# A Nyström attention and MLP kernel: its prologue re-ordered on all engines, W1 split over two engines, each output store cut into two of 64 rows

## The chip, the cores and the metric

The kernel runs on one NeuronCore of a Trainium2 chip. The metric is the device time of one execution in microseconds (us), as the median of several runs. The profile is of one further execution; times inside it count from the start of its span.

## The reference, cut to what matters

q, k and v are [8 batches, 8 heads, 576 rows, 64]. Each head uses 32 landmark rows (means over 18 rows) and a six-step iteration for an inverse; the eight heads' results are joined to x of [8, 576, 512], on which a layer norm and an MLP work.

```python
A, Bm, C = sm(q, k_lm), sm(q_lm, k_lm), sm(q_lm, k)
for _ in range(6):
    Z = 2 * Z - Z @ Bm @ Z
attn = A @ Z @ C @ v
...
xn = (x - mu) / np.sqrt(var + 1e-06) * g_ln
ch = np.maximum(xn @ w_ch1, 0.0) @ w_ch2
return x + ch
```

w_ch1 (W1) is [512, 2048] and w_ch2 (W2) is [2048, 512].

## The kernel before, in words

**Attention.** `attention(b)` is a generator: it emits one batch's attention in pieces and yields between them. Its inputs come by six loads of 576 KB each on SP's queue (`load`: q and k for two sets of four heads, then v), are cast to fp16 (`nat`, `natv`; by DVE, ACT and POOL for batch 0, by POOL for the rest), transposed on PE into `pst` and copied out as `xT`; `pss` holds the landmark sums (nine matmuls against the 0/1 matrix `pm16`). From `pss` DVE makes `klm` and `qbd`. Then come `psb` (landmark scores), its exponential `ebm`, the normalised `bm16`, its transpose `bmT`, then `psc`/`ect`, `psse`/`cmx`, `pscv`, six iterations of `psn` on PE and `st` on DVE (two `psa`/`ea` beside them), `pszc`, the two `zcbd`, and last five blocks of rows: `psy` on PE, `rcpd` and `xblk` on DVE. `block_done` takes the statistics of each finished block of 128 rows (`st6`, `mvg`) and, when four are there (a group), the layer norm: `lnv` and `rstd` on ACT, then four `xn`.

**MLP.** `mlp()` is a second generator, one step for each matmul. For each of nine groups it transposes `xn` (`psxt`, copied out by DVE as `xnT`), does 64 matmuls `psh` (16 column tiles of W1, `hT` is their ReLU, by ACT) and 64 matmuls `pso`; DVE adds x (`ot`), and `store` sends 256 KB to DRAM by one DMA, or two of 64 rows where a batch boundary falls into the block.

**Order.** PE runs in exactly the order written: the main loop takes one piece of attention, then `fill` takes some MLP matmuls. Batch 1's attention (`a1`) begins inside that of batch 0 (`a0`). The other engines' order comes from the scheduler, except DMA issues, which are pinned by `keep_in_program_order`. ACT, DVE, POOL and SP each run their list in order, so what waits holds what is behind it. W1 arrives in eight column blocks of 512 KB through `w1stg` (two buffers) on SP's queue, and ACT multiplies each by g in four operations (line 172); W2 arrives by four DMAs on POOL's queue that cast on the way (line 176). `psM` is a pool of three PSUM banks for `psh`, `pso`, `psxt` and, for one batch, the small attention tiles.

Of the kernel before, what the change touches and what calls it, by code (L numbers as in the profile page):

```python
# [15 lines left out]
P = 128  # L16
# [3 lines left out]
def kernel(  # L20
# [37 lines left out]

    def MM(o, l, r, rb=0, cb=0, start=True, stop=True, skip=False):
# [16 lines left out]
    def cast(eng, out_, in_):  # L76
        if eng == "act":
            nc.scalar.activation(out_, in_, AF.Copy)
        elif eng == "dve":
            nc.vector.tensor_copy(out=out_, in_=in_)  # L80
        else:
            nc.gpsimd.tensor_copy(out=out_, in_=in_)  # L82


    def load_qk(b, engines):
        tiles = {}
        for u in range(U):
            for (nm, src) in (("q", q), ("k", k)):
                tiles[nm, u] = load(src, b, u)
        out_ = {}  # L90
        for key, eng in zip(tiles, engines):
            t = nat.tile([P, NJ, 2, D], FP16, name="nat", tag="nat")
            cast(eng, t[:].rearrange("p j r d -> p r j d"), tiles[key][:])
            out_[key] = t
        return out_

    def load_v(b, engines):
        natv = natv_buf[b % NV]
# [66 lines left out]
    w1_stg = []  # L165

    def load_w1(i):
        stg = wstage.tile([P, KCH, W1N], FP32, name="w1stg", tag="w1stg")
        tc.keep_in_program_order(
            nc.sync.dma_start(out=stg[:], in_=w1_src[:, :, ts(i, W1N)]))  # L170
        for c in range(KCH):
            nc.scalar.activation(w1_16[:, c, ts(i, W1N)], stg[:, c, :], AF.Copy,  # L172
                                 scale=g_sb[:, c:c + 1])
# [30 lines left out]
    def attention(b):  # L204
        nt = nat_tiles.pop(b)
        natv = v_tiles.pop(b)
        zcbd = zcbd_buf[b % NV]
        pool1, tag1 = (psM, "pm") if b == 1 else (ps1, "p1")
# [44 lines left out]
        ebm = asm.tile([P, U, LM], FP32, name="ebm", tag="ebm")  # L253
        nc.scalar.activation(ebm[:], psb[:], AF.Exp, scale=sc_B)
# [13 lines left out]
        for u in range(U):  # L268
# [6 lines left out]
            nc.scalar.activation(t[:], psc[:], AF.Exp, scale=sc_C)  # L275
# [3 lines left out]
        psse = p1([P, 2, U, LM], "psse")  # L279
# [242 lines left out]
```

## Time and profile before

| | us |
|---|---|
| median of 3 runs (lowest, highest) | 393.53 (393.42, 395.13) |
| the profiled execution's own time | 391.23 |
| its span | 389.5 |
| PE busy in the span | 344.7 (89%) |
| DVE, ACT, POOL busy | 170.0, 129.7, 82.1 |

The span is what the trace covers; 1.73 us of the execution lie around it. PE is the busy engine, but a share over the whole span hides three stretches: a prologue in which PE mostly waits, a long stretch in which it hardly does, and an end without PE.

### The profile page before, as it was taken

What the parts mean: (1) busy time and instruction counts of PE and PEld (TensorE: products, weight loads), DVE (VectorE), ACT (ScalarE), POOL (GpSimd) and SP (SyncE); (2) the same over time, 40 slices, a digit from 0 to 9 for tenths busy, and PEclk for the clock granted to TensorE, in tenths of its full rate; (3) what the DMA queues carried; (4) which work ended last, traced back from release to release, by engine and by line L of the source; (5) the groups of instructions that cost most, each with busy time, mean ns of one, the idle gap of its engine ahead of it and who ended that gap; (6) DMA issues with size and microseconds to landing.
All of it is one profiled execution on the core that took longest, in us unless ns stands there. A gap on an engine that the chain in (4) does not pass through costs nothing.

```text
span 389.5 us, 8220 instructions
## 1 busy us (share of the span) xinstructions
PE 344.7 (89%) x3528; PEld 175.7 (45%) x3528; DVE 170.0 (44%) x431; ACT 129.7 (33%) x240; POOL 82.1 (21%) x100
## 2 busy tenths in 40 slices
PE   1796299799999999999999999999999999999940
PEld 1663045344554464446444644464444444444410
DVE  0548368635734574466347634852491210210110
ACT  2325854410551046014601450255027016016000
POOL 2750048500090009003600350300030210000000
PEclk9998679999999999999999999999999999999985
DMA  7999499201821191019111900100020011020011
GB/s 294 395 216 245 161 334 393 74 15 53 316 95 29 45 339 65 21 51 354 52 46 33 364 34 26 51 34 3 29 60 22 14 51 44 14 72 23 14 51 42
DMA packets 24755, 44.55 MB, mean 114 GB/s; under 512 B 1680, under 2 KB 7824, under 8 KB 24720
## 3 DMA queue, kind: packets, MB, share of 16 engines
q1 hardware_dynamic: 22608, 41.95, 30.5%
q0 software_dynamic: 2112, 2.10, 3.4%
q8 instruction: 27, 0.44, 0.5%
q14 instruction: 8, 0.07, 0.0%
HBM read 36.70 MB, written 9.44 MB: 118 GB/s over the span
## 4 chain that ended last, share of the span: by engine, by line
PE 82%; DVE 6%; DMA 4%; ACT 2%; issue 1%; POOL 1%; SPq 0%
PE pso L61 33%; PE psh L61 31%; PE pst L66 5%; DMA w1stg<-in_moe_w_ch_dram 2%; PE pss L61 2%; PE psn L61 2%; PE psy L61 2%; PE psxt L66 2%; ACT w L172 2%; DMA stg<-in_q_dram 2%; PE psa L61 2%; DVE ot L459 1%; DVE bm L260 1%; PE pscv L61 1%; PE psc L61 1%
## 5 line engine op out<-in xcount | busy, mean ns | idle before, releaser
L448 ACT ACTIVATE hT<-psh 128x512 f16<-128x512 f32 x144 | 85.7, 597 | 159.8 <-PE psh L61 159.8
L61 PE MATMUL psh<-xnT,w 128*128 128x512 f16 x576 | 137.5, 380 | 0.2 <-DVE xnT L427 0.2
L61 PE MATMUL pso<-w,hT 128*128 128x512 f16 x576 | 135.8, 380 | 0.2 <-DVE xnT L427 0.2
L61 PEld LDWEIGHTS <-hT 128*128 128x128 f16 x576 | 53.1, 98 | 60.2 <-issue 3.3
L61 PEld LDWEIGHTS <-w 128*128 128x128 f16 x576 | 52.9, 98 | 54.8 <-issue 2.1
L459 DVE TENSOR_TENSOR ot<-pso,xblk 128x512 f32<-128x512 f32 x36 | 24.8, 689 | 80.5 <-PE pso L61 80.5
L402 POOL TENSOR_SCALAR xn<-xblk,rstd,negmr 128x512 f16<-128x512 f32 x34 | 26.2, 785 | 138.2 <-DVE negmr L397 62.9
L82 POOL CAST nat<-stg 128x1152 f16<-128x1152 f32 x29 | 32.9, 1148 | 88.1 <-DMA stg<-in_q_dram 49.8
L324 DVE SCALAR_TENSOR_TENSOR st<-st,psn 128x192 f16<-128x192 f16 (+1 forms) x48 | 16.4, 342 | 48.6 <-PE psn L61 48.6
L66 PE MATMUL pst<-ident,nat 128*128 128x128 f16 x288 | 24.6, 239 | 6.7 <-DVE nat L80 5.4
L231 DVE COPY xT<-pst 128x1152 f16<-128x1152 f16 x28 | 21.1, 755 | 19.2 <-PE pst L66 19.2
L367 DVE TENSOR_TENSOR xblk<-psy,rcpd 128x512 f32<-128x512 f32 (+1 forms) x40 | 27.3, 684 | 0.7
L66 PEld LDWEIGHTS <-nat 128*128 128x128 f16 x288 | 20.9, 107 | 13.5 <-DVE nat L80 5.4
L388 DVE BATCH_NORM_STATS2 st<-xblk 128x6 f32<-128x512 f32 x36 | 24.5, 681 | 0.4
L82 POOL CAST natv<-stg 128x1152 f16<-128x1152 f32 x16 | 18.3, 1153 | 3.7 <-DMA stg<-in_v_dram 3.7
L66 PE MATMUL psxt<-ident,xn 128*128 128x128 f16 x144 | 12.9, 228 | 6.5 <-DVE xn L402 4.1
L61 PE MATMUL pss<-pm,nat 128*128 128x64 f16 x288 | 15.4, 204 | 3.5 <-POOL pm L114 3.5
L61 PE MATMUL psy<-zcbd,ea 128*128 128x260 f16 (+1 forms) x80 | 16.3, 287 | 1.8 <-DVE xblk L367 1.2
L338 ACT ACTIVATE ea<-psa 128x576 f16<-128x576 f32 x16 | 10.4, 650 | 18.3 <-PE psa L61 18.3
L172 ACT ACTIVATE w<-w1stg,g_sb 128x256 f16<-128x256 f32 x32 | 13.4, 496 | 5.1 <-DMA w1stg<-in_moe_w_ch_dram 5.1
L61 PEld LDWEIGHTS <-nat 128*128 128x128 f16 x288 | 13.3, 106 | 3.7 <-issue 3.7
L66 PEld LDWEIGHTS <-xn 128*128 128x128 f16 x144 | 9.9, 101 | 10.3 <-DVE xn L402 4.3
(63 smaller groups left out, 170.3 us busy)
## 6 DMA issues: line engine op xcount, KB each, us to landing
stg<-in_q_dram SPq DMA_DIRECT2D x16, 576.0 KB
stg<-in_k_dram SPq DMA_DIRECT2D x16, 576.0 KB
stg<-in_v_dram SPq DMA_DIRECT2D x16, 576.0 KB
out_dram<-ot SPq DMA_DIRECT2D x32, 256.0 KB
w1stg<-in_moe_w_ch_dram SPq DMA_DIRECT2D x8, 512.0 KB
w<-in_moe_w_ch_dram POOLq DMA_DIRECT2D x4, 512.0 KB, 9.2
out_dram<-ot SPq DMA_DIRECT2D x8, 128.0 KB
g_sb<-in_moe_g_ln_dram SPq DMA_DIRECT2D x1, 2.0 KB
```

Source lines behind the costliest of these rows:

```text
L61: nc.tensor.matmul(o, l, r, start=start, stop=stop, tile_position=(rb, cb), skip_group_check=(skip or cb != 0)))
L66: nc.tensor.matmul(o, i_, idn, is_transpose=True, tile_position=(0, 0)))
L82: nc.gpsimd.tensor_copy(out=out_, in_=in_)
L172: nc.scalar.activation(w1_16[:, c, ts(i, W1N)], stg[:, c, :], AF.Copy, scale=g_sb[:, c:c + 1])
L231: nc.vector.tensor_copy(out=t[:], in_=pst[:])
L324: nc.vector.scalar_tensor_tensor(out=stn[:, :, lo:], in0=st[:, :, lo:], scalar=2.0, in1=psn[:, :, lo:], op0=ALU.mult, op1=ALU.subtract)
L338: nc.scalar.activation(t[:], psa[:].rearrange("p j t -> p (j t)"), AF.Exp, scale=sc_A)
L367: nc.vector.tensor_tensor(out=xb[rows, :].rearrange("s (u h e) -> s u h e", u=U, e=D), in0=py[:, :, :, 0:D], in1=rcpd[rows, :, :, None].br ...
L388: nc.vector.bn_stats(out=st6[:], in_=x_blk[j][:])
L402: eng.tensor_scalar(out=xn[:], in0=x_blk[4 * g + i][:], scalar1=rstd[:, i:i + 1], scalar2=negmr[:, i:i + 1], op0=ALU.mult, op1=ALU.add)
L448: nc.scalar.activation(hT[:, m, :], psh[:], AF.Relu)
L459: nc.vector.tensor_tensor(out=ot[:], in0=pso[:], in1=x_blk.pop(j)[:], op=ALU.add)
```

## The change

- Batch 0's q and k are all cast by DVE, its first three `xT` are copied by ACT, and POOL's masks and `pm16` come ahead of its first cast. For the last of the four tiles the sums `pss` come before the transposes.
- `ebm` overwrites `psb` in PSUM, and `cmx` lies in PSUM too. `negmr` is gone: `xn` subtracts the mean and multiplies by `rstd`. Group 0's four `xn` are all DVE's.
- W1 has four staging buffers; of a block's four multiplications ACT does two and POOL two. Blocks 0 to 4 are asked for in the prologue, 5 to 7 and three of W2's DMAs inside the first group's `psh`. While `early` holds, ACT's and POOL's operations are pinned in the written order (`pin`).
- Batch 1's attention starts later in that of batch 0, so the first `psh` comes before batch 1's `psb`. Batch 1's small tiles use `ps1`, batch 0's `psM`.
- Batch 2's loads go through POOL's queue, batch 3's follow at once on SP's.
- Every store is two DMAs of 64 rows. `psxt` and `xnT` are no longer done in one piece of four between two `pso` tiles: one goes behind each eighth matmul of the last two.

```diff
-        tc.keep_in_program_order(nc.sync.dma_start(
+        queue = nc.gpsimd if b == 2 else nc.sync
+        tc.keep_in_program_order(queue.dma_start(
...
-    nat_tiles = {0: load_qk(0, ("dve", "act", "pool", "dve"))}
+    nat_tiles = {0: cast_batch(0, raw0, "dve")}
+    nat_tiles[1] = cast_batch(1, load_batch(1))
...
-    wstage = ctx.enter_context(tc.tile_pool(name="wstage", bufs=2))
+    wstage = ctx.enter_context(tc.tile_pool(name="wstage", bufs=4))
...
         for c in range(KCH):
-            nc.scalar.activation(w1_16[:, c, ts(i, W1N)], stg[:, c, :], AF.Copy,
-                                 scale=g_sb[:, c:c + 1])
+            dst = w1_16[:, c, ts(i, W1N)]
+            if c < KCH // 2:
+                pin(nc.scalar.activation(dst, stg[:, c, :], AF.Copy, scale=g_sb[:, c:c + 1]))
+            else:
+                pin(nc.gpsimd.tensor_scalar(out=dst, in0=stg[:, c, :], scalar1=g_sb[:, c:c + 1],
+                                        scalar2=None, op0=ALU.mult))
...
-        pool1, tag1 = (psM, "pm") if b == 1 else (ps1, "p1")
+        pool1, tag1 = (psM, "pm") if b == 0 else (ps1, "p1")
...
+                last = (u, i) == (U - 1, 1)
+                if last:
+                    sums()
...
-        ebm = asm.tile([P, U, LM], FP32, name="ebm", tag="ebm")
-        nc.scalar.activation(ebm[:], psb[:], AF.Exp, scale=sc_B)
+        ebm = psb
+        pin(nc.scalar.activation(ebm[:], psb[:], AF.Exp, scale=sc_B))
...
-            eng = nc.vector if (g == 0 and i % 2 == 0) else nc.gpsimd
+            eng = nc.vector if g == 0 else nc.gpsimd
             eng.tensor_scalar(out=xn[:], in0=x_blk[4 * g + i][:],
-                              scalar1=rstd[:, i:i + 1], scalar2=negmr[:, i:i + 1],
-                              op0=ALU.mult, op1=ALU.add)
+                              scalar1=mvg[:, i, 0:1], scalar2=rstd[:, i:i + 1],
+                              op0=ALU.subtract, op1=ALU.mult)
...
-            nc.sync.dma_start(out=rows[t0 // 64:(t0 + n) // 64], in_=ot[ds(p0, n), :])
+            for i in range(n // 64):
+                nc.sync.dma_start(out=rows[t0 // 64 + i], in_=ot[ds(p0 + 64 * i, 64), :])
...
+                if g == 0 and m % 2 == 0 and m < 6:
+                    load_w1(5 + m // 2)
+                    load_w2(4 + 2 * m)
...
+                    if u >= 2 and m % 8 == 3:
+                        if g + 1 in ln_ready and g + 1 not in xnTs:
+                            tr = transposes(g + 1)
+                        if tr is not None:
+                            next(tr, None)
...
-                if u >= 1 and g + 1 in ln_ready and g + 1 not in xnTs:
-                    for _ in transposes(g + 1):
-                        yield True
...
     for i, _ in enumerate(a0):
-        if i == 5:
-            for w in range(HID // W1N):
-                load_w1(w)
-            for m in range(0, MCH, 4):
-                load_w2(m)
-        if i >= 9:
+        if 10 <= i <= 14:
             next(a1)
+        if i in (16, 17, 18):
+            load_w1(i - 16)
+    for _ in range(4):
+        next(a1)
+    load_w1(3)
+    load_w1(4)
+    load_w2(0)
...
+        nat_tiles[2] = cast_batch(2, load_batch(2))
+        nat_tiles[3] = cast_batch(3, load_batch(3))
...
-            nat_tiles[b + 1] = load_qk(b + 1, ("pool",) * 4)
-            v_tiles[b + 1] = load_v(b + 1, ("pool",) * 2)
...
+        if 1 < b and b + 2 < B:
+            nat_tiles[b + 2] = cast_batch(b + 2, load_batch(b + 2))
```

ACT's list in the prologue, before, from the first W1 block to the first `hT` (a row with x8 is two blocks):

```order
L172 ACTIVATE w_16_147<-w1stg,g_sb 128x256 x8
L275 ACTIVATE ect<-psc 128x576
L172 ACTIVATE w_16_147<-w1stg,g_sb 128x256 x8
L338 ACTIVATE ea<-psa 128x576 x2
L393 ACTIVATE lnv<-mvg,eps_ln 128x4
L172 ACTIVATE w_16_147<-w1stg,g_sb 128x256 x8
L395 ACTIVATE rstd<-lnv 128x4
L172 ACTIVATE w_16_147<-w1stg,g_sb 128x256 x8
L448 ACTIVATE hT<-psh 128x512 x7
```

and the same stretch after it, where x4 is ACT's half of two blocks:

```order
L360 ACTIVATE ea<-psa 128x576 x2
L181 ACTIVATE w_16_147<-w1stg,g_sb 128x256 x4
L415 ACTIVATE lnv<-mvg,eps_ln 128x4
L417 ACTIVATE rstd<-lnv 128x4
L181 ACTIVATE w_16_147<-w1stg,g_sb 128x256 x6
L275 ACTIVATE psb<-psb 128x64
L296 ACTIVATE ect<-psc 128x576 x2
L468 ACTIVATE hT<-psh 128x512
```

Before, six blocks of W1 stood ahead of `rstd`; now two half blocks do, and the other blocks stand behind it.

DVE's list before, from batch 0's last block to the copy that lets the first `psh` go (numbers tell tiles of one name apart):

```order
L367 TENSOR_TENSOR xblk_924<-psy_925,rcpd_928 64x512
L324 SCALAR_TENSOR_TENSOR st_973<-st_940,psn_964 128x192
L397 SCALAR_TENSOR_TENSOR negmr_892<-mvg_739,rstd_890 128x4
L402 TENSOR_SCALAR xn_894<-xblk_732,rstd_890,negmr_892 128x512
L402 TENSOR_SCALAR xn_898<-xblk_846,rstd_890,negmr_892 128x512
L427 COPY xnT_975<-psxt_976 128x4x128
L427 COPY xnT_975<-psxt_982 128x4x128
```

and the same stretch after the change:

```order
L411 BN_AGGR mvg_569<-st6_612 128x2
L248 COPY xT_659<-pst_649 128x1152
L421 TENSOR_SCALAR xn_619<-xblk_562,mvg_569,rstd_617 128x512
L421 TENSOR_SCALAR xn_621<-xblk_573,mvg_569,rstd_617 128x512
L421 TENSOR_SCALAR xn_623<-xblk_589,mvg_569,rstd_617 128x512
L421 TENSOR_SCALAR xn_625<-xblk_605,mvg_569,rstd_617 128x512
L447 COPY xnT_698<-psxt_699 128x4x128
L248 COPY xT_709<-pst_683 128x1152
L447 COPY xnT_698<-psxt_711 128x4x128
L447 COPY xnT_698<-psxt_717 128x4x128
L258 CAST klm_723<-pss_484 128x128
L260 TENSOR_TENSOR qbd_725<-pss_484,mask2_93 128x256
```

In both, more `xnT` copies follow (two before, one after). The list now has four `xn` in place of two, and two `xT` copies, `klm` and `qbd` of batch 1, which stood far ahead before, among them.

POOL's list before, from batch 1's last casts to batch 2's:

```order
L82 CAST natv_111<-stg 128x18x64 x2
L176 DMA w_16_148<-in_moe_w_ch_dram 128x4x512 x4
L402 TENSOR_SCALAR xn<-xblk,rstd,negmr 128x512 x2
L82 CAST nat<-stg 128x2x9x64 x4
L82 CAST natv_105<-stg 128x18x64 x2
```

and the same stretch after the change:

```order
L89 CAST natv_107<-stg 128x18x64 x2
L183 TENSOR_SCALAR w_16_147<-w1stg,g_sb 128x256 x10
L187 DMA w_16_148<-in_moe_w_ch_dram 128x4x512
L183 TENSOR_SCALAR w_16_147<-w1stg,g_sb 128x256 x2
...
L187 DMA w_16_148<-in_moe_w_ch_dram 128x4x512
L78 DMA stg<-in_q_dram 128x2x576
...
L78 DMA stg<-in_v_dram 128x2x576 x2
L89 CAST nat<-stg 128x2x9x64 x4
L89 CAST natv_101<-stg 128x18x64 x2
```

Batch 2's six loads now stand on POOL's queue behind half of W1's multiplications and all of W2's DMAs.

## Rows read from the trace of the kernel before

**Rows 1.** Windows: busy us of each engine (instructions), PE clock, DMA share, GB/s.
```profile
0.00:52.00 52.00, 28.02 (x548) 20.10 (x549) 25.80 (x74) 24.21 (x47) 17.37 (x32) 0.88 0.89 264
52.00:374.65 322.65, 316.71 (x2980) 155.56 (x2979) 143.53 (x357) 105.45 (x194) 64.68 (x68) 1.00 0.27 93
374.65:389.50 14.85, 0.00 (x0) 0.00 (x0) 0.69 (x1) 0.00 (x0) 0.00 (x0) 0.58 0.12 45
```

**Rows 2.** Chain that ended last, 0 to 60 us: start, length, what.
```profile
33.86 5.23 DMA w1stg<-in_moe_w_ch_dram
...
52.01 1.44 PE psh L61 x4
```

**Rows 3.** Timeline, ACT: start, length, operation, idle before it and releaser.
```profile
44.55 0.30 ACT L393 ACTIVATE lnv<-mvg,eps_ln 128x4 f32<-128x4 f32 x1 [0.19 <-DVE mvg L389]
...
48.38 0.19 ACT L395 ACTIVATE rstd<-lnv 128x4 f32<-128x4 f32 x1
```

**Rows 4.** Waits of PE: for whom, us in total, times, longest.
```profile
PE pss L61 <- POOL pm L114: 3.5, 1, 3.5
PE psse L61 <- DVE bmT L263: 3.2, 2, 2.5
PE psxt L66 <- DVE ot L459: 2.3, 7, 0.3
```

**Rows 5.** Timeline of the prologue and of batch 1's last blocks.
```profile
0.81 0.45 SPq L71 DMA_DIRECT2D stg<-in_q_dram  x1
...
16.30 0.41 DVE L239 TENSOR_TENSOR qbd<-pss,mask 128x256 f16<-128x256 f32 x1
...
20.92 0.35 PE L61 MATMUL psn<-st 32*32 32x96 f16 x8 [0.60 <-DVE st L309]
...
21.79 0.35 PE L61 MATMUL psn<-st 32*32 32x96 f16 x8
...
21.85 1.15 POOL L82 CAST natv<-stg 128x1152 f16<-128x1152 f32 x1 [0.53 <-DMA stg<-in_v_dram]
...
57.07 0.21 DVE L366 RECIPROCAL rcpd<-psy 128x8 f32<-128x8 f32 x1
...
61.26 0.18 DVE L366 RECIPROCAL rcpd<-psy 128x8 f32<-128x8 f32 x1
```

**Rows 6.** Groups of instructions by form: count, busy us, mean ns, idle before.
```profile
L231 DVE COPY xT<-pst 128x1152 f16<-128x1152 f16 x28 | 21.1, 755 | 19.2 <-PE pst L66 19.2
L427 DVE COPY xnT<-psxt 128x512 f16<-128x512 f16 x36 | 13.1, 416 | 0.2
L402 POOL TENSOR_SCALAR xn<-xblk,rstd,negmr 128x512 f16<-128x512 f32 x34 | 26.2, 785 | 138.2 <-DVE negmr L397 62.9 <-PE psy L61 35.2 <-DVE rcpd L366 21.0
```

**Rows 7.** Two tiles, xn and bm: shortest, median and longest ns.
```profile
L402 DVE TENSOR_SCALAR xn<-xblk,rstd,negmr x2: 547/736/926, 48.8 to 49.3; 128x512 f16<-128x512 f32 x2
...
L260 DVE TENSOR_TENSOR bm<-ebm,rcr x8: 224/542/3950, 17.8 to 262.2; 128x64 f16<-128x64 f32 x8
```

**Rows 8.** Chain that ended last, 100 to 128 us (batch 3 at full clock).
```profile
109.67 0.69 PE psc L61 x36
...
114.20 0.69 PE pscv L61 x72
...
116.72 0.19 PE psn L61 x8
116.91 0.35 PE psa L61 x8
```

**Rows 9.** DMA in GB/s by slices: 0 to 8, 346 to 354 (0.2 us), 374 to 390 (0.4 us).
```profile
GB/s 0 0 0 0 0 0 0 0 0 92 219 323 369 438 392 253 300 334 380 380 357 403 392 415 392 369 300 323 334 357 346 403 369 357 438 369 311 380 380 357
...
GB/s 41 61 41 61 41 61 41 61 41 61 41 61 41 143 82 92 82 174 164 215 256 215 82 123 82 102 102 92 41 61 41 61 41 61 41 61 41 61 41 61
...
GB/s 51 51 51 51 51 51 51 51 51 51 51 51 51 51 51 51 51 51 51 51 51 46 51 51 51 51 51 51 51 51 51 51 51 51 36 0 0 0 0 0
```

**Rows 10.** DMA issues: engine, count, KB each, median us to landing.
```profile
w<-in_moe_w_ch_dram POOLq DMA_DIRECT2D x4, 512.0 KB, 9.2
```

More of the change, by code (lines that the diff above doesn't have):

```diff
@@ L77, in cast @@
         if eng == "act":
-            nc.scalar.activation(out_, in_, AF.Copy)
+            pin(nc.scalar.activation(out_, in_, AF.Copy))
         elif eng == "dve":
@@ L81, in cast, with load_batch, cast_batch @@
         else:
-            nc.gpsimd.tensor_copy(out=out_, in_=in_)
-    def load_qk(b, engines):
+            pin(nc.gpsimd.tensor_copy(out=out_, in_=in_))
+    def load_batch(b):
         tiles = {}
         for u in range(U):
-            for (nm, src) in (("q", q), ("k", k)):
-                tiles[nm, u] = load(src, b, u)
-        out_ = {}
[L91 to L98, printed above, removed]
-        for u in range(U):
-            stg = load(v, b, u)
-            cast(engines[u], natv[:, 2 * u:2 * u + 2, :, 0:D], stg[:])
-        return natv
-    nat_tiles = {0: load_qk(0, ("dve", "act", "pool", "dve"))}
+            tiles["q", u] = load(q, b, u)
+            tiles["k", u] = load(k, b, u)
+        for u in range(U):
+            tiles["v", u] = load(v, b, u)
+        return tiles
+    def cast_batch(b, tiles, eng_qk="pool"):
+        natv = natv_buf[b % NV]
+        out_ = {}
+        for u in range(U):
+            for nm in ("q", "k"):
+                t = nat.tile([P, NJ, 2, D], FP16, name="nat", tag="nat")
+                cast(eng_qk, t[:].rearrange("p j r d -> p r j d"), tiles[nm, u][:])
+                out_[nm, u] = t
+        for u in range(U):
+            cast("pool", natv[:, 2 * u:2 * u + 2, :, 0:D], tiles["v", u][:])
+        return out_, natv
+    raw0 = load_batch(0)
     ident16 = const.tile([P, P], FP16, name="ident16")
@@ L221, in attention, with sums @@
                 pst = p2([P, NJ, P], FP16, "pst")
+                def sums():
+                    for j in range(NJ):
+                        MM(pss[:, i, u, :], n16[:, j, :, :].rearrange("p r d -> p (r d)"),
+                           pm16[:], start=(j == 0), stop=(j == NJ - 1), skip=True)
+                last = (u, i) == (U - 1, 1)
+                if last:
+                    sums()
                 for j in range(NJ):
                     TR(pst[:, j, :], n16[:, j, :, :].rearrange("p r d -> p (r d)"), ident16[:])
-                for j in range(NJ):
-                    MM(pss[:, i, u, :], n16[:, j, :, :].rearrange("p r d -> p (r d)"), pm16[:],
-                       start=(j == 0), stop=(j == NJ - 1), skip=True)
+                    if b == 1 and j == 4:
+                        yield 1
                 t = aprep.tile([P, NJ, P], FP16, name="xT", tag="xT")
-                if b < 2 and nm == "k":
-                    nc.scalar.copy(t[:], pst[:])
+                if b == 0 and not last:
+                    pin(nc.scalar.copy(t[:], pst[:]))
                 else:
@@ L232, in attention @@
                 xT[nm, u] = t
+                if not last:
+                    if b == 1:
+                        yield 1
+                    sums()
                 yield 2
@@ L461, in mlp, with next_loads @@
                 yield True
-                if u >= 1 and g + 1 in ln_ready and g + 1 not in xnTs:
-                    for _ in transposes(g + 1):
-                        yield True
+            if tr is not None:
+                for _ in tr:
+                    yield True
     stream = mlp()
+    w_done = []
+    def next_loads():
+        if len(w_done) < HID // W1N:
+            return False
+        nat_tiles[2] = cast_batch(2, load_batch(2))
+        nat_tiles[3] = cast_batch(3, load_batch(3))
+        return True
     def fill(n):
@@ L489 @@
             fill(n if b == 1 else 2 * n)
+            if b == 1 and early[0] and next_loads():
+                early[0] = False
+        if b == 1 and early[0]:
+            raise ValueError("the first group starts too late")
+        if 1 < b and b + 2 < B:
+            nat_tiles[b + 2] = cast_batch(b + 2, load_batch(b + 2))
     for _ in stream:
```

40 lines of the change are left out of this document (19 added, 21 removed).

## The prediction

> **What bounds the kernel now.** I read the windows first, cut where PE's character changes [rows 1]. In the first 52.0 us PE is busy for 28.0. From there to 374.65 it is busy for 316.7 of 322.65: this stretch is PE's own and gets shorter only by the 5.9 us of waits in it. In the last 14.85 us PE does nothing and DVE one `ot` of 0.69. So a change can win at both ends and, in the middle, little.
>
> The start ends with the first `psh`, at 52.01 [rows 2]. ACT's timeline shows what holds it: `lnv` is done at 44.85, but `rstd`, which needs nothing else, starts at 48.38 [rows 3], since ACT runs its list in order and two blocks of W1 stand between. Those wait for staging: one wait for a block is 5.23 us long [rows 2]. Ahead of that lies batch 0's attention, a chain of small operations whose first `psn` starts at 20.92 [rows 5]; PE's longest wait in it is 3.5 us for `pm16` [rows 4], which POOL finishes behind a cast.
>
> The end is a queue of stores. In the last 15 us the DMA moves a flat 51 GB/s, while loads move 300 to 400 [rows 9]; 256 KB at 51 GB/s are 5.1 us, and several were in line. The one place before it with a store in two of 64 rows reaches 256 GB/s [rows 9].
>
> **The start, step by step.** I follow the new chain to the first `psh`.
>
> 1. *To the first `psn`.* Batch 0's loads are unchanged. They move some 365 GB/s from 1.8 us on [rows 9], so the fourth tile (4 x 590 kB) is moved at 8.3 and landed, I estimate, near 9.6. DVE casts it by 10.4; `pss` comes ahead of its transposes, so `qbd` can start near 11.5, where it started at 16.30 [rows 5]. From `qbd` to `psn` it was 4.6 us. In that stretch `bm` waited; in its short form it takes 0.22 [rows 7], but `rsum` now queues behind an `xT` copy, so I keep 4.7. First `psn` at 16.2: 4.7 us earlier.
> 2. *The six iterations.* Two `psn` were 0.87 us apart [rows 5]: 5.2 for six. The two `psa`, batch 1's transposes put between, `pszc` and the two `zcbd` add, I estimate, 1.8: the first `psy` near 23.3.
> 3. *Five blocks.* One `xT` copy of 0.76 [rows 6] and the `psy` itself, then `rcpd`, which repeated every 1.4 us (three steps from 57.07 to 61.26 [rows 5]). With the half block ahead of the last statistics that is about 6.8: `mvg` at 30.8.
> 4. *Layer norm.* `lnv` and `rstd` (0.30 and 0.19 [rows 3]) run beside an `xT` copy of 0.76, then come four `xn` of 0.74 (shortest 0.55, longest 0.93 [rows 7]). Behind them DVE's list has four `xnT` of 0.42, one `xT` of 0.76 [rows 6], `klm` and `qbd` of at most 0.41 each [rows 5]: 3.2. The first `psh` comes at 30.8 + 0.8 + 2.6 + 3.1 = **37.3**, where it was 52.01: **-14.7**. All `xn` at their longest, W1's half blocks of POOL in between (below) and a looser chain make it 40; all at the shortest and batch 0 without gaps 35.
>
> *Cover of W1.* The first `psh` needs one block. Batch 1's last load landed by 21.85 [rows 5]; block 0 follows it in the queue and no W2 DMA competes. At 300 to 400 GB/s a block takes 1.3 to 1.8 us, so four are there by 29. POOL's half multiplication is not in the trace: above nothing and below the 0.785 of a `xn` with twice the elements [rows 6]; at the upper end a block costs POOL 1.6, as long as its transfer. Ten are done by about 31.5, so I take 0 for the path; without that cover `xn` waits up to 1.6, which is in the 40. ACT's share of blocks 2 to 7 is now late behind `rstd`, but block 2 is first needed four tiles (16 `psh`) later.
>
> *Work moved past the first `psh`.* Batch 1 has done less by then. Still to come at full clock are `psc` 0.69, `pscv` 0.69, five `psn` of 0.19 and two `psa` of 0.35 [rows 8], with `psb` and `psse` estimated at 0.4 together: **+3.5**.
>
> **The middle.** PE waited 2.5 us at one stroke for `bmT` [rows 4]; the `bm` ahead of it took 3.95 us instead of 0.22 [rows 7], while POOL cast without a pause. With `ebm` in PSUM `bm` is like `qbd`, which reads PSUM beside one SBUF operand and keeps to 0.41: **-2.5** (none of it if POOL holds such an operation too). The seven waits of `psxt` for `ot`, 2.3 us [rows 4], go, as no `psxt` follows a `pso` directly. What is late next is the last `xnT` (0.42, perhaps behind a longer DVE operation) against four `pso`; I charge 0.5 (0 to 2.3, all given back): **-1.8**.
>
> The skill speaks against one part here. What the row shows is a `bm` of 224/542/3950 ns beside a busy POOL [rows 7]. By the Trainium skill ("SBUF — State Buffer", Who interferes with whom) VectorE's operations with two SBUF inputs or in a two-port mode share a port pair with GpSimd under an exclusive lock. The trace agrees for `bm`. By that rule the four `xn` now on DVE are exposed to POOL's half of W1; it is the first rival below.
>
> **The end.** After the last matmul: `ot` 0.69 [rows 1], two issues of 0.45, one us from an issue to its bytes (issue at 0.81 [rows 5], bytes from 1.8 [rows 9]), 128 KB twice, and 1.5 from the last byte to the end (388.0 to 389.5 [rows 9, 1]). The pair of 64-row stores took under 3 us with the slow ones still running beside it, at its peak 256 GB/s [rows 9]: bounds 1.0 and 3.0, partly under the issue; I take 1.1 past the second issue. Sum 5.2, from 4.7 to 7, in place of 14.85: **-9.7**.
>
> The skill has a rule against this edit as well. What the rows show is 51 GB/s for whole stores and up to 256 for a pair of halves [rows 9]. By the Trainium skill ("DMA: Bandwidth & Descriptors", Rules for kernel authors) two transfers to disjoint partition halves serialize on the same engines and one of 128 partitions is to be preferred; by that rule the end would stay at 14.85 plus one issue. The trace does not agree for these shapes.
>
> **Sum.** -14.7 + 3.5 - 2.5 - 1.8 - 9.7 = **-25.2**. The profiled execution took 391.23, so 366.0. The median of before lies 2.3 above its profiled execution; I carry that over: **368.3**. The bounds of the terms give 363 to 375.
>
> **Rivals.**
> - *DVE and POOL in each other's way.* Group 0's chain is DVE's alone now. If its `xn` wait out POOL's runs as that `bm` did, each can lose up to 3.7 us; two such waits move the start by 7: 375. For it: `bm`'s 3.95. Against: POOL pauses for each block of W1 to land.
> - *The stores gain nothing.* The end stays 14.85 + 0.45: 378.5. For it: two DMAs cost SP two issues. Against: the peak at the pair.
> - *New waits in the PE stretch.* Batch 2's data come behind W2 on POOL's queue. W2's last DMA is issued near 40 by my estimate and lands 9.2 later [rows 10]; loads of 1.5 us each behind it bring q and k in by 55 and v by 58, each with a cast of some 1.2. PE wants the first tile some 19 us after the first `psh`, near 56, the last near 60. W2 slower by 6 to 10 us than that makes waits of about 6: 374.
> - *Slower than before.* W2's DMAs took 9.2 us each to land [rows 10]. If batch 2's six loads, on the same queue, went one after another at that pace from 42 us on, the sixth would land at 97, PE would want it (`pscv`) near 67 and lose 30 us: 398. It decides from about 8.4 us a load. Against: loads in flight together share the full 300 to 400 GB/s on SP's queue [rows 9], and nothing in the rows says that POOL's cannot.
> - *Better.* Start at 35 and every wait gone: 363.5.
>
> **How the numbers follow.** The forecast as worked out (363 to 373) 0.72; DVE and POOL 0.09; stores 0.04; new PE waits 0.09; slower 0.03; better than 363: 0.03. The range of 363 to 376 leaves out the stores' rival, the slow one and the ends. Half a per cent, about 2 us, is what this kernel's runs can tell from no change; all but the slow case lie beyond it: faster 0.96, same 0.01, slower 0.03.
>
> **What would show it.** Right: the first `psh` between 35 and 40; `rstd` directly behind `lnv`; no `bm` above 0.3; at the end some 5 us without PE and a DMA rate over 200 GB/s; from the first `psh` to the last `ot` about 323 us. Wrong: `xn` over 1 us, PE waiting for `nat` of batch 2 or for `xnT`, a flat 51 GB/s at the end.

## The result, and the profile after

The changed kernel takes 363.83 us (median of 4 runs, 362.82 to 364.48) against 394.33 for the kernel before on the same chip: ratio 0.9222, 95% interval [0.9184, 0.9261]. In a second comparison it was 0.9176 [0.9152, 0.9200]. The forecast was 368.3 (363 to 376), faster. The profiled execution took 363.58, its span is 361.8.

The windows of the changed kernel, cut as those of before were [rows 1]: at the first `psh`, at the last `ot`, to the end. Columns: length, then busy time (instructions) of PE, weight loads, DVE, ACT, POOL, then granted clock, DMA share, GB/s.

```profile
0.00:36.78 36.78, 23.51 (x367) 16.56 (x368) 22.90 (x63) 12.05 (x21) 23.27 (x39) 0.77 0.88 305
36.78:356.56 319.78, 318.98 (x3161) 156.97 (x3160) 145.35 (x364) 109.49 (x201) 116.15 (x81) 0.99 0.36 103
356.56:361.80 5.24, 0.00 (x0) 0.00 (x0) 0.69 (x1) 0.00 (x0) 0.00 (x0) 0.96 0.22 52
```

The start is shorter by 15.2 us, the middle by 2.9, the end by 9.6. In the middle PE now idles for 0.8 us, where it idled for 5.9: it is PE's own stretch, but for its clock.

ACT's timeline answers to [rows 3]. `rstd` follows `lnv` at once, and three half blocks of W1 come behind both:

```profile
31.17 0.30 ACT L415 ACTIVATE lnv<-mvg,eps_ln 128x4 f32<-128x4 f32 x1 [4.32 <-DVE mvg L411]
31.50 0.20 ACT L417 ACTIVATE rstd<-lnv 128x4 f32<-128x4 f32 x1
31.61 2.49 ACT L181 ACTIVATE w<-w1stg,g_sb 128x256 f16<-128x256 f32 x6
```

From there DVE's list sets the first `psh`, which waits 1.8 us for the last row here:

```profile
31.74 2.48 DVE L421 TENSOR_SCALAR xn<-xblk,mvg,rstd 128x512 f16<-128x512 f32 x4
34.14 0.40 DVE L447 COPY xnT<-psxt 128x512 f16<-128x512 f16 x1
34.47 0.74 DVE L248 COPY xT<-pst 128x1152 f16<-128x1152 f16 x1
35.13 0.74 DVE L447 COPY xnT<-psxt 128x512 f16<-128x512 f16 x2
35.79 0.27 DVE L258 CAST klm<-pss 128x128 f16<-128x128 f32 x1
35.99 0.41 DVE L260 TENSOR_TENSOR qbd<-pss,mask 128x256 f16<-128x256 f32 x1
36.32 0.41 DVE L447 COPY xnT<-psxt 128x512 f16<-128x512 f16 x1
```

Every `bm` is short now (before 224/542/3950 ns, [rows 7]), and POOL's `xn` has become long (785 ns before, [rows 6]). First the view of the tile `bm` (shortest, median, longest in ns), then POOL's groups (busy us, mean ns of one):

```profile
L281 DVE TENSOR_TENSOR bm<-psb,rcr x8: 224/224/225, 13.6 to 252.4; 128x64 f16<-128x64 f32 x8
```
```profile
L421 POOL TENSOR_SCALAR xn<-xblk,mvg,rstd 128x512 f16<-128x512 f32 x32 | 66.0, 2072 | 63.6 <-DVE xblk L389 31.3 <-ACT rstd L417 21.9 <-PE psxt L72 9.0
...
L183 POOL TENSOR_SCALAR w<-w1stg,g_sb 128x256 f16<-128x256 f32 x16 | 14.8, 939 | 0.7 <-DMA w1stg<-in_moe_w_ch_dram 0.5
```

The DMA view of the last stretch, 346 to 362 us in 40 slices, answers to the flat 51 GB/s of [rows 9]: each block is a short burst, and the queue is empty between two.

```profile
GB/s 0 0 0 0 0 200 195 205 56 0 0 0 0 56 205 215 174 5 0 0 0 0 143 184 225 103 0 0 0 0 0 225 184 220 46 0 0 0 0 20
```

### The profile page after: what moved, and what is told of

It reads as the page before. It is cut to its first block, busy times and chain, and to the rows that moved or that the text cites. A ratio compares the mean times of both kernels' runs of the same rounds, so it can differ in the third digit from the quotient of the medians.

```text
span 361.8 us, 8266 instructions
## 1 busy us (share of the span) xinstructions
PE 342.5 (95%) x3528; PEld 173.5 (48%) x3528; DVE 168.9 (47%) x427; ACT 121.5 (34%) x222; POOL 139.4 (39%) x119
## 4 chain that ended last, share of the span: by engine, by line
PE 83%; DMA 8%; POOL 6%; SPq 1%; issue 1%; DVE 0%; POOLq 0%
PE pso L67 36%; PE psh L67 32%; POOL w L183 4%; PE pst L72 3%; DMA stg<-in_k_dram 3%; DMA stg<-in_v_dram 3%; DMA w1stg<-in_moe_w_ch_dram 3%; PE psxt L72 2%; PE psy L67 2%; PE psn L67 2%; PE pss L67 2%; PE psa L67 1%; PE psc L67 1%; PE pscv L67 1%; SPq L78 1%; POOL w L187 1%
## 5 line engine op out<-in xcount | busy, mean ns | idle before, releaser
L67 PE MATMUL psh<-xnT,w 128*128 128x512 f16 x576 | 139.2, 381 | 1.8 <-DVE xnT L447 1.8
L67 PE MATMUL pso<-w,hT 128*128 128x512 f16 x576 | 138.8, 380 | 0.0
L421 POOL TENSOR_SCALAR xn<-xblk,mvg,rstd 128x512 f16<-128x512 f32 x32 | 66.0, 2072 | 63.6 <-DVE xblk L389 31.3
L67 PEld LDWEIGHTS <-hT 128*128 128x128 f16 x576 | 51.6, 98 | 54.1 <-issue 2.4
L72 PE MATMUL pst<-ident,nat 128*128 128x128 f16 x288 | 25.7, 241 | 6.6 <-DVE nat L87 6.0
L72 PEld LDWEIGHTS <-nat 128*128 128x128 f16 x288 | 20.6, 108 | 12.0 <-DVE nat L87 6.4
L447 DVE COPY xnT<-psxt 128x512 f16<-128x512 f16 x36 | 15.1, 423 | 23.5 <-PE psxt L72 23.5
L183 POOL TENSOR_SCALAR w<-w1stg,g_sb 128x256 f16<-128x256 f32 x16 | 14.8, 939 | 0.7 <-DMA w1stg<-in_moe_w_ch_dram 0.5
L67 PEld LDWEIGHTS <-st 32*32 32x32 f16 x384 | 5.7, 90 | 19.3 <-issue 11.1
L72 PEld LDWEIGHTS <-xn 128*128 128x128 f16 x144 | 10.9, 100 | 7.9 <-issue 0.7
## 6 DMA issues: line engine op xcount, KB each, us to landing
stg<-in_k_dram POOLq DMA_DIRECT2D x2, 576.0 KB, 10.8
```

Source lines behind the costliest of these rows:

```text
L72: nc.tensor.matmul(o, i_, idn, is_transpose=True, tile_position=(0, 0)))
L183: pin(nc.gpsimd.tensor_scalar(out=dst, in0=stg[:, c, :], scalar1=g_sb[:, c:c + 1], scalar2=None, op0=ALU.mult))
L421: eng.tensor_scalar(out=xn[:], in0=x_blk[4 * g + i][:], scalar1=mvg[:, i, 0:1], scalar2=rstd[:, i:i + 1], op0=ALU.subtract, op1=ALU.mult)
L447: nc.vector.tensor_copy(out=xnT[:, :, ts(u, P)], in_=psxt[:])
```

## The experiments

Eleven edited kernels ran, and the changed one once more. A note for reading them: the first `psn` comes anywhere from 14.4 to 16.2 us in executions of kernels whose beginning is the same, so where a start is compared I count from the first `psn` to the first `psh` (20.9 us in the changed kernel, 20.95 in its second profile). The three columns on the right are of one profiled execution each. All but the edit shown is kept in each.

| kernel | us, median (lowest to highest) | first `psh` | from it to the last `ot` | from that to the end |
|---|---|---|---|---|
| before (its profile) | 394.33 (393.42 to 395.57) | 52.01 | 322.64 | 14.85 |
| changed | 363.83 (362.82 to 364.48) | 36.78 | 319.78 | 5.24 |
| changed, again | 362.34 (360.92 to 363.52) | 36.73 | 319.76 | 5.31 |
| 1 before, halves | 385.56 (385.08 to 385.99) | 53.02 | 325.73 | 5.05 |
| 2 changed, whole stores | 372.06 (371.64 to 372.34) | 35.74 | 319.87 | 14.89 |
| 3 W1 early in the order | 372.29 (372.26 to 373.3) | 45.43 | 319.86 | 5.31 |
| 4 W1 on ACT alone | 371.09 (370.58 to 372.23) | 35.56 | 328.60 | 5.24 |
| 5 before, new beginning | 394.99 (393.66 to 396.69) | 53.02 | 325.06 | 14.92 |
| 6 `ebm` in SBUF | 364.7 (363.11 to 367.86) | 35.76 | 325.07 | 5.37 |
| 7 transposes together | 372.13 (370.82 to 373.12) | 35.94 | 327.91 | 5.25 |
| 8 `xT` on ACT | 362.22 (360.12 to 364.24) | 36.96 | 320.58 | 4.96 |
| 9 old form of `xn` | 364.19 (one run) | 36.31 | 321.05 | 4.94 |
| 10 two operations for W1 | 362.04 (one run) | 35.21 | 319.84 | 5.25 |
| 11 candidate | 361.83 (360.5 to 362.44) | 35.01 | 318.41 | 5.38 |

### 1 and 2. The stores alone, put in and taken out

```diff
-            nc.sync.dma_start(out=rows[t0 // 64:(t0 + n) // 64], in_=ot[ds(p0, n), :])
+            for i in range(n // 64):
+                nc.sync.dma_start(out=rows[t0 // 64 + i], in_=ot[ds(p0 + 64 * i, 64), :])
```

> The kernel before, with nothing changed but the stores: each is two DMAs of 64 rows. My theory: a whole store moves 51 GB/s and a pair of halves some 200, so the queue at the end goes and with it 9 to 10 us: ratio 0.975 to 0.977 (about 384.7 against 394.3), first psh still near 52, the end without PE near 5 us. Rival (the shorter end of the changed kernel comes from its other parts, and halves only cost issues): ratio 1.000 to 1.002, and the end stays near 15 us.

In the other direction:

> The changed kernel with whole stores again, all else kept. My theory: the end is back to 14.5 to 15 us in place of 5.3, and the time is 373 to 374 (9 to 10 us above the changed kernel's 363.8, ratio near 0.947). Rival (the end is set by how the last group's work lies and not by the stores): 364 to 365.

Measured: ratio to before 0.9763 [0.9739, 0.9787] with halves put in, as expected. With whole stores the changed kernel takes 372.06, less than the 373 to 374 expected: it loses 8.2 us by the medians (not measured side by side) and 9.65 in the stretch itself, while its first `psn` came 1.3 earlier than in the changed kernel's profile. The last window of each, halves in the kernel before and whole stores in the changed one:

```profile
378.75:383.80 5.05, 0.00 (x0) 0.00 (x0) 0.69 (x1) 0.00 (x0) 0.00 (x0) 1.00 0.23 54
```
```profile
355.61:370.50 14.89, 0.00 (x0) 0.00 (x0) 0.69 (x1) 0.00 (x0) 0.00 (x0) 0.65 0.12 46
```

The end is the stores' and nothing else's: it goes with the edit in either kernel. What to read in the second row is the DMA share: 0.12 of 16 engines is the work of two engines, at some 50 GB/s together. The packets of the trace say the same: two are in flight for 10.7 of the 12.0 us from 357 to 369, while in the changed kernel, in the 1.39 us in which any are between 357.5 and 361, it is eleven or more for 1.16. A whole store's DRAM side has an outermost size of two (two rows of j, each of 64 x 2 KB). By the Trainium skill ("DMA: Bandwidth & Descriptors", Rules for kernel authors) an outermost dimension of a size below 16 confines a DMA to at most that many engines. The trace agrees: 0.12 x 16 = 1.9. It is not the rule that the prediction weighed, and it fits this edit where that one did not.

### 3. W1's place in ACT's list

```diff
-        if i in (16, 17, 18):
-            load_w1(i - 16)
+        if i == 5:
+            for w in range(3):
+                load_w1(w)
```

> The changed kernel with its first three W1 blocks put early in the written order (at the fifth piece of batch 0's attention), so that their multiplications stand ahead of ea in ACT's pinned list; the split over ACT and POOL and all else are kept. My theory: ACT waits at its head for blocks that land at 24 to 28 us, ea and with it the iterations' end and psy come late, first psh at 41 to 46, total 368 to 374. Rival (place in the list does not matter, as the loads themselves are issued no later): first psh near 37, total 363.5 to 364.5.

Measured: 372.29, first `psh` at 45.43, 30.2 us behind the first `psn` in place of 20.9. As expected, and the rival falls. The blocks stand in another place than before the change: there they held batch 1's `ea` and `rstd`, here batch 0's `ea`. ACT's timeline; the number in brackets is the idle time ahead:

```profile
24.35 0.91 ACT L181 ACTIVATE w<-w1stg,g_sb 128x256 f16<-128x256 f32 x2 [10.60 <-DMA w1stg<-in_moe_w_ch_dram]
25.78 0.91 ACT L181 ACTIVATE w<-w1stg,g_sb 128x256 f16<-128x256 f32 x2 [0.53 <-DMA w1stg<-in_moe_w_ch_dram]
27.25 0.91 ACT L181 ACTIVATE w<-w1stg,g_sb 128x256 f16<-128x256 f32 x2 [0.57 <-DMA w1stg<-in_moe_w_ch_dram]
28.07 1.17 ACT L360 ACTIVATE ea<-psa 128x576 f16<-128x576 f32 x2
```

ACT idles 10.6 us for a block, with two finished `psa` behind it. PE waits 9.7 us for `ea`, and the rest of the attention is late by as much.

### 4. W1 on ACT alone

```diff
-            if c < KCH // 2:
+            if c < KCH:
```

> The changed kernel with all four multiplications of each W1 block on ACT and none on POOL; their places in the order are kept. My theory: what moved the start is where W1's work stands in ACT's list, not that POOL shares it. ACT has only some 0.45 us for each of the 10 operations that it takes over, five blocks arrive at 24 to 34 us, and two of them stand ahead of lnv at most: first psh between 36.5 and 38.5 (36.8 in the changed kernel), total 363.5 to 365.5. Rival (the split is what frees ACT): lnv and rstd wait for three blocks of ACT work, first psh 40 to 43, total 367 to 370.

Measured: 371.09. The start does not suffer: first `psh` at 35.56 (36.5 to 38.5 expected), 20.2 behind the first `psn`, 0.7 less than in the changed kernel, since four `xn` on DVE take 1.91 us without POOL's W1 beside them in place of 2.48. The total that I drew from it is too low by 5.6 us or more: they are lost in the middle, 8.8 us longer by the profile. ACT and PE there:

```profile
52.21 1.71 ACT L181 ACTIVATE w<-w1stg,g_sb 128x256 f16<-128x256 f32 x4 [3.74 <-DMA w1stg<-in_moe_w_ch_dram]
53.82 1.54 ACT L468 ACTIVATE hT<-psh 128x512 f16<-128x512 f32 x3
```
```profile
54.45 0.59 PE L67 MATMUL psh<-xnT,w 128*128 128x512 f16 x1 [4.47 <-ACT hT L468]
54.97 0.29 PE L67 MATMUL psn<-st 32*32 32x64 f16 x8
55.19 1.89 PE L67 MATMUL psh<-xnT,w 128*128 128x512 f16 x4
```

W1's last block stands between the `hT` in ACT's list, ACT waits for its data, and PE waits 6.0 us in two strokes for `hT`. After the second one four `psh` take 1.89 us, where the changed kernel has 1.04 at the same place: they ran at the lower of the clock's two levels (granted clock 0.50, 1.2 GHz, from 54.45 to 59.05 us; 1.00 in the changed kernel). Why is the block late? It is asked for at 34.3, as in the changed kernel (33.4), but lands after up to 17.9 us in place of 10.2. The DMA issues on POOL's list tell it, in this experiment and then in the changed kernel:

```profile
23.67 3.22 POOL L187 DMA_DIRECT2D w<-in_moe_w_ch_dram  x4
26.84 0.76 POOL L78 DMA_DIRECT2D stg<-in_q_dram  x1
```
```profile
33.89 0.96 POOL L187 DMA_DIRECT2D w<-in_moe_w_ch_dram  x1
...
42.67 0.72 POOL L78 DMA_DIRECT2D stg<-in_q_dram  x1
```

With no W1 to multiply, POOL issues W2's four loads at 24 us and batch 2's from 27 us on, some 10 to 16 us earlier, into the time in which W1's blocks want the DMA. So the split's worth lies less in sharing the arithmetic than in holding these loads back. That reading is from two traces; a run with W1 on ACT and POOL's loads held back was not made.

### 5. The new beginning alone in the kernel before

```diff
-    nat_tiles = {0: load_qk(0, ("dve", "act", "pool", "dve"))}
+    raw0 = {(nm, u): load(src, 0, u) for u in range(U) for nm, src in (("q", q), ("k", k))}
...
+    nat_tiles = {0: {}}
+    for key, raw in raw0.items():
...
+        cast("dve", t[:].rearrange("p j r d -> p r j d"), raw[:])
...
-                if b < 2 and nm == "k":
+                if (b == 0 and not last) or (b == 1 and nm == "k"):
```

The sums `pss` of the last tile also stand ahead of its transposes, as in the changed kernel.

> The kernel before with one part of the change alone: batch 0's q and k are all cast by DVE, POOL's masks and pm16 come ahead of its casts, the first three xT are copied by ACT, and pss comes ahead of the transposes for the last tile. W1, layer norm, stores and the interleaving stay as they were. My theory: the first psn comes 4 to 6 us earlier, at 15 to 17 (20.9 before), but the first psh gains little of it, since lnv and rstd still stand behind W1 blocks that wait for staging in ACT's list: first psh at 49 to 52 (52.0 before), total 0 to 3 us less than before. Rival (the parts of the start add up): first psh 47 to 48, total 4 to 5 us less.

Measured: ratio 1.0011 [0.9988, 1.0035], no change. The first `psn` comes at 16.22, where the forecast had it, and nothing of that arrives: the first `psh` is at 53.02, even later than the 49 to 52 expected. (Before's own beginning gave a first `psn` at 20.92 in its profile and at 19.07 in experiment 1, whose first `psh` is at 53.02 too.) ACT's timeline shows who takes it:

```profile
40.06 1.70 ACT L177 ACTIVATE w<-w1stg,g_sb 128x256 f16<-128x256 f32 x4 [8.31 <-DMA w1stg<-in_moe_w_ch_dram]
...
46.01 0.30 ACT L401 ACTIVATE lnv<-mvg,eps_ln 128x4 f32<-128x4 f32 x1 [0.19 <-DVE mvg L397]
46.22 3.28 ACT L177 ACTIVATE w<-w1stg,g_sb 128x256 f16<-128x256 f32 x8
49.41 0.19 ACT L403 ACTIVATE rstd<-lnv 128x4 f32<-128x4 f32 x1
```

Batch 1's `ea` is behind that wait of 8.31 us (PE waits 9.1 for it), `rstd` behind eight more multiplications. The parts of the start don't add up: the early attention is worth nothing while W1 is loaded and multiplied as before. The change moved W1 in ACT's list, doubled its staging buffers and delayed W2's loads; no run takes these apart. In before's trace W1's loads waited 15.9 us for ACT to free one of the two buffers, so the buffers can be part of it.

### 6. `ebm` in SBUF again

```diff
-        ebm = psb
+        ebm = asm.tile([P, U, LM], FP32, name="ebm", tag="ebm")
```

> The changed kernel with ebm in an SBUF tile again, so that bm has two SBUF operands; all else kept. My theory: beside POOL's casts, and its xn which are longer now, some bm take several us instead of 0.22; batches whose bm falls into a busy stretch of POOL stall PE at psse: longest bm above 1 us, 1 to 8 us more PE waiting, total 364.5 to 372. Rival (with the new order POOL is not running when bm does, so the place of ebm does not matter): all bm at 0.22 to 0.30, total 363.3 to 364.3.

Measured: 364.7, four runs from 363.11 to 367.86; the times alone don't separate it from the changed kernel. The profile does, and it is of the slowest of the four: the longest `bm` is 3.5 us, and PE waits 4.0 us for `bmT` in place of 0.4.

```profile
L281 DVE TENSOR_TENSOR bm<-ebm,rcr x8: 224/712/3536, 12.6 to 256.7; 128x64 f16<-128x64 f32 x8
```

Two stretches between the last `ot` of two groups are longer by 1.5 and 3.8 us than in the changed kernel, the others the same. The two longest `bm` (2.83 and 3.54 us) lie in rows of POOL casts without a pause. That the stall comes in some executions and not in others would fit the spread of the four times, but only one was profiled. With the operand in PSUM no `bm` is above 0.226 us in any profile.

### 7. Transposes in one piece

```diff
-                    if u >= 2 and m % 8 == 3:
-                        if g + 1 in ln_ready and g + 1 not in xnTs:
-                            tr = transposes(g + 1)
-                        if tr is not None:
-                            next(tr, None)
-                            yield True
...
+                if u >= 1 and g + 1 in ln_ready and g + 1 not in xnTs:
+                    for _ in transposes(g + 1):
+                        yield True
```

> The changed kernel with psxt and xnT of the next group in one piece of four between two pso tiles, as before; all else kept. My theory: each of seven or eight groups waits some 0.3 us for ot again, PE's waits of psxt for ot come to 1.8 to 2.4 us, total 1.5 to 2.5 us above the changed kernel of the same call. Rival (the waits only move, as pso behind them starts later but its other waits shrink): within 0.5 us. Second rival (POOL's longer xn are late when the piece stands earlier): 3 us or more above.

Measured: 372.13 against 362.34 of the changed kernel run beside it, +9.8 (by the profiles the middle is +8.1). Both my theory and the second rival happen, in different places. From the end of group 0 on the middle is longer by 3.2 us (278.51 against 275.31): PE's idle time, nearly all of it waits for `ot`, makes 1.4 of it, and the rest is PE's own, since sixteen `psxt` in one piece take longer than four times four between `pso`. PE in this experiment, then in the changed kernel:

```profile
298.28 0.61 PE L72 MATMUL psxt<-ident,xn 128*128 128x128 f16 x8
299.22 0.71 PE L72 MATMUL psxt<-ident,xn 128*128 128x128 f16 x8 [0.34 <-DVE ot L483]
299.89 3.40 PE L67 MATMUL pso<-w,hT 128*128 128x512 f16 x15
```
```profile
75.46 0.39 PE L72 MATMUL psxt<-ident,xn 128*128 128x128 f16 x4
75.68 1.46 PE L67 MATMUL pso<-w,hT 128*128 128x512 f16 x6
```

A piece holds PE for 1.61 us, 0.34 of it waiting; spread, four starts cost 0.22 each until the next `pso`, 0.9 in all. The other 4.9 us come ahead of group 0's end: the piece stands earlier, and POOL's `xn` of 2.07 us aren't done:

```profile
72.51 0.40 PE L72 MATMUL psxt<-ident,xn 128*128 128x128 f16 x4 [1.20 <-POOL xn L421]
74.57 0.49 PE L72 MATMUL psxt<-ident,xn 128*128 128x128 f16 x4 [1.66 <-POOL xn L421]
...
75.85 3.02 PE L67 MATMUL pso<-w,hT 128*128 128x512 f16 x8
```

Waits of 2.9 us are followed by slow work: eight `pso` take 3.02 us, 1.90 a few us later, and the granted clock is 0.83 from 70 to 80 us (1.00 in the changed kernel).

### 8. Batch 1's last `xT` on ACT

```diff
-                if b == 0 and not last:
+                if (b == 0 and not last) or (b == 1 and u == U - 1):
```

> The changed kernel with the last two xT copies of batch 1 on ACT instead of DVE; in DVE's list klm and qbd then stand ahead of group 0's xn and no xT stands between xn and xnT. My theory: PE's 1.8 us wait of the first psh for xnT is DVE's list, so some of it goes: first psh at 34.8 to 36.0 (36.8 in the changed kernel), total 362.0 to 363.3. Rival (the wait is for the last xn and xnT themselves, or ACT's copies push lnv back by as much): first psh 36.5 to 37.5, total 363.5 to 364.8.

Measured: 362.22 (360.12 to 364.24), no difference to be told; the first `psh` is 20.85 behind the first `psn`, as in the changed kernel. The 1.8 us of waiting for `xnT` is down to 0.5, and 1.7 have come up at `psxt`, which waits for `xn`. DVE's list has `klm` first, and it is `klm` that waits:

```profile
32.01 0.29 DVE L258 CAST klm<-pss 128x128 f16<-128x128 f32 x1 [0.85 <-PE pss L67]
32.22 0.41 DVE L260 TENSOR_TENSOR qbd<-pss,mask 128x256 f16<-128x256 f32 x1
32.55 2.92 DVE L421 TENSOR_SCALAR xn<-xblk,mvg,rstd 128x512 f16<-128x512 f32 x4
```

`rstd` was done at 31.7, and `xn` starts at 32.55. My theory falls: the wait has moved, and the first `psh` is where the rival had it (36.96).

### 9 and 10. What makes POOL slow

```diff
-                              scalar1=mvg[:, i, 0:1], scalar2=rstd[:, i:i + 1],
-                              op0=ALU.subtract, op1=ALU.mult)
+                              scalar1=rstd[:, i:i + 1], scalar2=negmr[:, i:i + 1],
+                              op0=ALU.mult, op1=ALU.add)
```

> The changed kernel with xn written as before: multiply by rstd, add -mean*rstd, with one small operation on DVE per group for that term. My theory: POOL's time for xn hangs on the pair of operations, so xn on POOL falls from 2.07 us to 0.75 to 0.85 and POOL's busy time from 139 to some 97 us; POOL is off the path, so the span stays at 361.3 to 362.3. Rival (xn is slow on POOL because of what runs beside it in the new order): xn stays near 2 us. Second rival (POOL's long xn costs PE time): the span falls by 2 us or more.

And for W1:

```diff
-                                        scalar2=None, op0=ALU.mult))
+                                        scalar2=0.0, op0=ALU.mult, op1=ALU.add))
```

> The changed kernel with POOL's multiplication of W1 written with a second operation, plus 0.0. My theory: the pair multiply, add runs at the pace that xn had before (0.785 us for 128x512), so a W1 operation of 128x256 falls from 0.94 us to 0.40 to 0.50, POOL is done with ten of them earlier, group 0's four xn on DVE meet fewer of them and come nearer to 0.55 each: first psh 36.0 to 36.6 in place of 36.8, span 361.0 to 361.8. Rival (a second operation costs POOL time): 1.2 us or more for each, first psh at 37 or later.

Measured: POOL's `xn` is back at 766 ns, and POOL's W1 operation falls from 939 to 493 ns. POOL's group in the one, then in the other:

```profile
L424 POOL TENSOR_SCALAR xn<-xblk,rstd,negmr 128x512 f16<-128x512 f32 x32 | 24.2, 766 | 86.5 <-DVE negmr L419 37.4 <-DVE mvg L411 31.6 <-PE psxt L72 17.5
```
```profile
L183 POOL TENSOR_SCALAR w<-w1stg,g_sb 128x256 f16<-128x256 f32 x16 | 7.7, 493 | 9.5 <-DMA w1stg<-in_moe_w_ch_dram 9.5
```

The pair of operations sets the pace, not the neighbours. (One run of each.) Some 42 us of POOL's time in the first gain nothing (364.19, span 362.3): POOL is off the path there. In the second the first `psh` is 20.7 behind the first `psn`, 0.2 less; the four `xn` on DVE take 603 ns each in place of 678, not the 0.55 us expected. The rest of its lower span is an earlier `psn` (14.50).

### 11. A candidate, and its yardstick

```diff
-                                        scalar2=None, op0=ALU.mult))
+                                        scalar2=0.0, op0=ALU.mult, op1=ALU.add))
...
-                if b == 0 and not last:
+                if (b == 0 and not last) or (b == 1 and last):
```

> A candidate: the changed kernel with POOL's W1 operation as multiply, add 0.0, and the last xT copy of batch 1 on ACT, so that DVE has no xT between xn and xnT. My theory: POOL's W1 operations are done early, xn meets fewer of them, and one xT copy of 0.74 us leaves the chain from rstd to the first psh: first psh 19.7 to 20.2 us behind the first psn (20.9 in the changed kernel), total 0.6 to 1.4 us below the changed kernel of the same call. Rival (ACT's copy stands behind W1 in its list and psc waits for it): within 0.3 us of the changed kernel.

> The changed kernel itself once more, as the yardstick for the two small edits beside it (transposes together; the candidate). Nothing is changed: 363 to 364.5 us, first psh 20.5 to 21.2 us behind the first psn.

Measured: 361.83 against 362.34 (the yardstick, itself below the 363 to 364.5 expected); to before 0.9164 [0.9141, 0.9186] against 0.9176 [0.9152, 0.9200]. The intervals overlap, so no gain is shown. The chain from `psn` to `psh` is 20.6 us, not the 19.7 to 20.2 that I expected: the `xT` has left it, but `xn` still takes 2.64. Its middle is 1.4 shorter by the profile, all of it in group 0, with a granted clock of 1.00 in the first 5 us behind the first `psh`; the changed kernel has 0.66 there in both profiles. The middle goes with that clock: 318.41 us at 1.00, 319.76 to 319.87 at 0.66 (the changed kernel twice, experiments 2, 3 and 10), 320.58 and 321.05 at 0.50 (experiments 8 and 9). One profile of each doesn't say whether an edit brought its clock.

## Why the prediction was right, point by point

**The start, -14.7: right, -15.2.** First `psn` forecast at 16.2, seen at 15.89; first `psy` 23.3 and 23.91; `mvg` 30.8 and 30.97; first `psh` 37.3 and 36.78. Step 1 was 0.3 long and step 3 0.4; step 2 was 0.9 short, as PE lost 1.2 us at a `psa`; step 4 was 0.7 long, most of it in DVE's list behind `xn` (2.56 instead of 3.1). So the closeness of the sum owes something to errors that cancel. Step 4 also took 2.6 for four `xn` of 0.74, which are 3.0, and 3.1 for the 3.2 behind them, without saying why; with its own figures it would have been 0.5 later. Experiment 3 shows that W1's place in ACT's list can cost this much (8.5 us there), and experiment 5 that step 1 alone is worth nothing; the buffers and W2's later loads were not tried apart from the place.

I read two rows of before wrongly. The 5.23 us is the time of a transfer in the chain, and not of a block between `lnv` and `rstd`. ACT idled 3.15 us for that block, ahead of batch 1's `ea`; between `lnv` and `rstd` it mostly worked:

```profile
39.11 3.30 ACT L172 ACTIVATE w<-w1stg,g_sb 128x256 f16<-128x256 f32 x8 [3.15 <-DMA w1stg<-in_moe_w_ch_dram]
...
44.76 1.69 ACT L172 ACTIVATE w<-w1stg,g_sb 128x256 f16<-128x256 f32 x4
46.77 1.71 ACT L172 ACTIVATE w<-w1stg,g_sb 128x256 f16<-128x256 f32 x4 [0.33 <-DMA w1stg<-in_moe_w_ch_dram]
```

And the 3.5 us for `pm16` is not PE's longest wait in batch 0's attention; the first cast is, with 5.4.

**W1's cover: its bound failed, and little came of it.** I bounded POOL's multiplication of 128x256 by the 0.785 of a `xn` with twice the elements. It took 0.939, since a `xn` was then in the faster pair of operations (experiment 10). Ten were done at 33.9, not 31.5, and cost the `xn` beside them 0.57 us (2.48 against 1.91). ACT alone (experiment 4) is 7 us worse, by two traces for a reason that the prediction did not have: POOL's work also delays POOL's loads.

**Work moved, and the `bm` stall: the stall right, the sum partly by luck.** From the first `psh` to the last `ot` of group 0 I had +3.5 - 2.5 - 0.3 = +0.7; by the two profiles it went from 44.16 to 44.47, +0.3. But these did not run at the same clock. The first 5 us behind the first `psh`, of before, of experiment 1 and of the changed kernel (granted clock third from the end):

```profile
52.01:57.01 5.00, 5.00 (x36) 1.97 (x36) 2.25 (x6) 3.28 (x7) 1.73 (x2) 0.91 1.00 345
```
```profile
53.02:58.02 5.00, 5.00 (x30) 1.53 (x29) 1.38 (x4) 3.01 (x7) 2.03 (x2) 0.68 1.02 379
```
```profile
36.78:41.78 5.00, 5.00 (x108) 2.48 (x110) 1.66 (x8) 3.26 (x7) 4.91 (x6) 0.66 1.05 169
```

Experiments 1 and 5 (0.68 and 0.73), with before's order there, need 46.79 and 46.57 us for the stretch. Against them the changed kernel is 2.1 to 2.3 us shorter, not 0.7 longer; which of the three terms is off stays open. No `bm` is above 0.225, and experiment 6 brings the stall back.

**The transposes, -1.8: the term that was mis-sized.** From group 0's end to the last `ot` it went from 278.48 to 275.31, -3.2; my share for that stretch was -1.5. The 0.5 charged for a late `xnT` was not due (no wait is left), and the 2.3 us of waits were not all that a piece costs: sixteen transposes at one place also hold PE longer than four times four (experiment 7, 3.2 us put back). And the spreading covers something that I had not seen coming, POOL's `xn` at 2.07 us: together the transposes meet them late, for 4.9 us more.

**The end, -9.7: right, -9.6** (experiments 1 and 2: -9.8 put in, +9.65 taken out).

**The sum.** -27.7 by the two profiles against -25.2, most of the gap being the middle. The other 2 us to the median are the 2.3 that I carried over from one kernel to the other: the changed kernel's profile lies at its median. Before's shown profile, 391.23, was faster than all its other runs but one (390.39), and two more with its order (experiments 1 and 5) have 53.0 and 325.1 to 325.7 where it has 52.0 and 322.6. By the medians of the comparison the change is worth 30.5 us, 5.3 more than forecast; 363.83 lies 0.8 above the lower end of the range, and the second comparison's 362.34 below it. From the first `psh` to the last `ot` my sum gave 321.9, not the 323 among the signs; it was 319.8.

**The rivals and signs.** One sign that I had set down as wrong came true, `xn` over 1 us: on POOL it is 2.07, by its pair of operations, and off the path. DVE and POOL in each other's way: there, but for 0.57 us of the 7. Stores: gone by experiment 1. Waits for batch 2: one, 0.4 us. One load after another on POOL's queue: no, q and k took 9.9 and 10.8 us to land, issued within 2.9 us of each other, the first cast at 51.96 and the fourth at 56.47. That batch's queue was not tried alone.

## What to carry to other kernels

In a list that an engine runs in order, first ask which entry waits for data, and what stands behind it: an earlier beginning was worth nothing while W1's blocks were handled as before, and 8.5 us hung on where three of them are written. Before you take work from an idle engine, look at what it will issue sooner: POOL without W1 started loads 10 to 16 us early, and PE lost 6 us waiting for work that, by two traces, these held up. Before you put a small difference down to an edit, compare the granted clock of the stretch in both profiles. And read a slow DMA's share of engines before its rate: 0.12 of 16 said that a whole store used about two engines, and cutting it so that 64 rows are outermost was worth 9.6 us at the end.

## What the runs showed of the hardware that I had not expected

- POOL's time for one instruction depends on its pair of operations: 128x512 takes 2072 ns as subtract, multiply and 766 as multiply, add; 128x256 takes 939 ns with one multiplication and 493 with a second operation added to it. More work in the instruction, half the time. On DVE the two forms of `xn` took 678 and 624 ns beside POOL's W1, and the first 540 without it.
- A wait can cost PE twice. After waits of 2.9 us in experiment 7 and 4.5 in experiment 4 its matmuls ran slowly for a while (eight `pso` 3.02 instead of 1.90 us, granted clock 0.68 from 75 to 80 us; four `psh` 1.89 instead of 1.04, clock 0.50), so that PE's busy time grew too: by 2.1 us in the stretch with the waits of experiment 7 and by 2.9 over the middle of experiment 4. Not every wait does: behind one of 1.5 us in experiment 4 four `psh` took 1.04.
